# Residual through the product, separate rstd groups and a new priority table in a two-block kernel

## The chip, the cores and the metric

The kernel runs on one core of a Trainium2 chip. The metric is the device time of one execution in microseconds (us); the number compared is the median of several runs. The engines are TensorE (PE in the profile, with its weight loads as PEld), VectorE (DVE), ScalarE (ACT), GpSimd (POOL) and the sync engine (SP), which issues most of the DMAs.

## What is computed

Two residual blocks over x of 2048 rows and 512 columns, in bf16. The first is linear attention with 32 heads of 16 columns, the second a gated MLP that mixes along the sequence:

```python
def _A_ref(x, wqkv, wo):
    q, k, v = ...                       # x @ wqkv, split in 32 heads of 16
    phi = lambda t: jnp.where(t > 0, t + 1, jnp.exp(t)) + 1e-06
    pq, pk = (phi(q), phi(k))
    kv = einsum('bhsd,bhse->bhde', pk, v); z = einsum('bhsd->bhd', pk)
    o = einsum('bhqd,bhde->bhqe', pq, kv) / (einsum('bhqd,bhd->bhq', pq, z)[..., None] + 1e-06)
    return merge_heads(o) @ wo
def _B_ref(x, w_in, w_sp, b_sp, w_out):  # F = 1792, Fh = 896
    z = gelu_tanh(x @ w_in); z1 = z[..., :Fh]; z2 = _layernorm(z[..., Fh:])
    g = einsum('ts,bsf->btf', w_sp, z2) + b_sp[None, :, None]
    return (z1 * g) @ w_out
h = x + _A_ref(_layernorm(x), A_wqkv, A_wo)
h2 = h + _B_ref(_layernorm(h), B_w_in, B_w_sp, B_b_sp, B_w_out)
```

## The kernel before

All of x, the weights and the intermediates stay in SBUF. The sequence is 16 tiles of 128 rows, eight pairs (p), four groups of 512 rows (gq or tg). PSUM is a pool of eight banks of 128 x 512 fp32; four of them hold the accumulator `acc` until the k·v sums are done.

The kernel is written as a list of operations (`op`), each with its engine, an estimated cost, what it reads and writes, and a priority. A list scheduler (`schedule`, L185) then fixes the order on each engine: at each step it takes, per engine, the candidates that can start soonest by the estimates, and among those that could start within a small patience (0.1 or 0.2 us) of the engine's being free, the one with the lowest priority number. `NUDGE` (L372) is a table of numbers that are added to the priorities in the order in which the operations are listed; operations past its end get nothing. So the order of everything on each engine, the sync engine's DMA queue among it, depends on the priorities, the table and the cost estimates. `_waits` derives the semaphores from the resulting order.

The stages in the order of time:

- *Start.* Loads of x, k's weights, v's and q's; the first five of the 64 transposed loads of w_sp (WSP0 = 5); ten products on zeros (`spin`, L617).
- *First layernorm* (L657 to L685). Per x tile: statistics (`stats`, L624), aggregate (`aggr`, L628); per group of tiles of `LN1` one rstd by ScalarE, Ln then Exp (`rstd_of`, L638 and L640); then the normalised tile by VectorE (`normalise`, L652) or ScalarE (L679). `LN1` has the groups [0], [1], [2, 3] and then fours.
- *Transposes of the normalised x* (`transpose_pair`, L689): pairs below XDMA = 2 by TensorE (L704) and a ScalarE copy out of PSUM (L715), the others by DMA transposes on the sync queue (L693). After the first one of tile 0 one product on zeros fills in (L711).
- *k and q* (`k_proj` L749, `q_proj` L783), each followed by `phi`: exp on ScalarE (L721), a VectorE pass (L725), and a last VectorE pass that either reads PSUM again (L737) or, for pairs below FR = 2, adds a ReLU that ScalarE wrote (L724, L736).
- *k·v* (L769): the products of the normalised x with phi(k), summed over all tiles in `acc`; for pairs below AS = 6 as one operation per tile, for later pairs as one operation per tile and half of the output (h).
- *Handover*: column sums of phi(k) (L804 to L821), the small products that make the merged matrix `mw` (L831 to L865), the denominators (`den`, L876 to L883), their spreading over columns (`spread_den`, L893 and L899), the scaling of phi(q) (`scale_pq`, L915 and L919).
- *h* (L937 to L967), in units: tiles 0 and 1 alone, then pairs. Four products per tile (L948), the residual added by VectorE straight from PSUM into the tile of x (L953), statistics, aggregate, rstd, normalised tile (L652). The rstd comes from ScalarE for units that begin below LNACT = 2 and from GpSimd (`rstd_pow`, L645 and L647) for the others. Tiles 0 and 1 are transposed by TensorE, the others by DMA (HDMA = 1).
- *Second block*: z2 (L976, Gelu at L985, statistics at L992 or L1000), z1 (L1021, L1026), the mixing product (L1051) with bias and gate on VectorE (L1057, L1060), the output product (L1071), residual (L1076) and store.

ScalarE uses two function tables: one with Ln and Exp at the start, one for Gelu. The list `last_lnexp` holds ScalarE's last Ln and Exp operations; all Gelus are listed after them.

Of the kernel before, what the change touches and what calls it, by code (L numbers as in the profile page):

```python
# [7 lines left out]
ACT = mybir.ActivationFunctionType  # L8
ALU = mybir.AluOpType

P = 128
# [98 lines left out]
class Program:  # L110
# [259 lines left out]


NUDGE = [  # L372
# [29 lines left out]
]  # L402


# [1 line left out]
def bass_sequential_preLN__linear_attn_block__mixer_gmlp__prompt_kernel(  # L406
# [16 lines left out]
    NT, KD, KF, NG = S // P, D // P, FH // P, S // GW  # L423
    TPG = GW // P
    NP = NT // 2
    assert D == 512 and KD == 4 and NG == 4 and FH == KF * P and 512 < FH <= 1024
    WARM, XDMA, HDMA, LNACT = 10, 2, 1, 2
    FILL = 1
    AS, FR, FQ, N0, WSP0 = 6, 2, 0, 4, 5
    WV, WQ, NA, KA, QE, QI = 8.5, 4, 1, 35, 3, 15  # L430
    WSP1 = 8
    DB, DC, SPP, PK, ZD = 6, 7, 8, 0.3, 1
# [23 lines left out]
    x = View(s_x, 0, [NT, D], BF16)  # L456
# [32 lines left out]
    ident = small([P], BF16)  # L489
# [34 lines left out]
    def bank(i):  # L524
        return lambda a: a[:, i, :]
# [11 lines left out]
    op = g.op  # L537
# [3 lines left out]
    def act_c(n, ps=True, ptr=0):  # L541
        return 0.15 + 0.00085 * n + 0.09 * ptr

    def dve_c(n, ps=True, mode=1):
        return 0.06 + 0.00112 * n / mode
# [108 lines left out]
           r=[src, m, rs], w=[dst], prio=prio)  # L654


    LN1 = [[0], [1], [2, 3], [4, 5, 6, 7], [8, 9, 10, 11], [12, 13, 14, 15]]  # L657
    last_lnexp = []
    xn_t = {}
    for grp in LN1:  # L660
# [94 lines left out]
    for p in range(NP):  # L755
# [5 lines left out]
        for h in ((None,) if p < AS else (0, 1)):  # L761
            for n in (2 * p, 2 * p + 1):
# [3 lines left out]
                def mm(e, n=n, l=l, hs=hs):  # L766
                    for g_ in hs:
                        for c in range(KD):
                            i = e.matmul(acc(xk(g_, c)).ap(), lhsT=l.ap()[:, c * P:(c + 1) * P],  # L769
                                         rhs=pk.ap[:, n, g_ * HW:(g_ + 1) * HW], start=False,  # L770
                                         stop=(n == NT - 1 and c % 2 == 1))
                    return i
# [165 lines left out]
    for u in UNITS:  # L938
        k, n0 = len(u), u[0]
        pr = B0 + 5 * n0  # L940
        scale_pq(u, pr - SCP, r0)
        t = Tile(PS, k)
        for ti, n in enumerate(u):
            l = pqT[:, n * P:(n + 1) * P]

            def mm(e, t=t, ti=ti, l=l):
                for c in range(KD):
                    i = e.matmul(t(bank(ti)).ap(), lhsT=l.ap()[:, c, :], rhs=mw[c, :].ap(), start=(c == 0),  # L948
                                 stop=(c == KD - 1))
                return i  # L950
            op("pe", 4 * MM, mm, r=[l, mw.all()], w=[t()], prio=pr)
        d = x[n0:n0 + k, :]
        op("dve", dve_c(512 * k), lambda e, t=t, d=d: e.tensor_tensor(d.ap(), t().ap(), d.ap(), ALU.add),  # L953
           r=[t(), d], w=[d], prio=pr)
        for n in u:
            stats(x[n, :], Row(st_h, n), pr + 1)
        for n in u:
            aggr(Row(st_h, n), 6, pr + 1)
        rs = small([k], FP32)
        var = st_h[n0:n0 + k, 7]  # L960
        if n0 < LNACT:
            last_lnexp.append(rstd_of(var, rs.all(), pr + 2))
        else:
            rstd_pow(var, rs.all(), pr + 2, k)
        for i, n in enumerate(u):
            t = hn_t[n] = Tile(XN)
            normalise(t(), x[n, :], Row(st_h, n), 6, rs[i:i + 1], pr + 3)  # L967
# [178 lines left out]
```

## Time and profile before

| what | value |
|---|---|
| median of 3 runs | 248.45 us (247.92 to 248.77) |
| the profiled execution's own time | 248.1 us |
| its span, first to last instruction | 246.4 us |
| VectorE, ScalarE, GpSimd busy | 129.6, 88.1, 27.0 us |
| HBM read, written | 7.47 MB, 2.10 MB |

All times in the profile are of one execution on the chip. L followed by a number is a line of the kernel. A name such as `xT_pq_z` is a buffer; buffers are shared by tensors that live at different times (xT, phi(q) and z1 here; the normalised x, phi(k) and z2 in `pk_xn_z`; q, k, v weights, the spread denominators and a part of w_sp in `wqkv_wsp`; x and later h in `xh`). In rows by groups, the number after the bar is busy time in us, then the mean of one instruction in ns, then the engine's idle time just before such instructions and what ended it. SPq means the sync engine's queue of DMA issues.

### The profile page before, as it was taken

Reading aid. Unit: us, or ns where it says so; the run is one execution under the profiler, and the core shown is the slowest. Engines: PE = TensorE matmul, PEld = TensorE weight load, DVE = VectorE, ACT = ScalarE, POOL = GpSimd, SP = SyncE. Lnnn points to the kernel's source line nnn. Section 1 sums busy time; section 2 is a strip of 40 time slices with the busy share of each in tenths; the row PEclk is TensorE's granted clock in tenths of the full one; section 3 lists DMA queues with packets and bytes.
Section 4 is the critical chain, followed back from the end, with each engine's and each line's share of the span. In section 5 each row is a group of like instructions: output and inputs, shape, how many; then the busy total and the mean of one; then the engine's idle time right before and its main releaser. Section 6 shows DMA issues by size and latency. Waiting matters only on the chain.

```text
span 246.4 us, 3157 instructions
## 1 busy us (share of the span) xinstructions
PE 238.0 (97%) x1220; PEld 115.7 (47%) x1242; DVE 129.6 (53%) x247; ACT 88.1 (36%) x132; POOL 27.0 (11%) x73
## 2 busy tenths in 40 slices
PE   7799999999899999999999999999999999999995
PEld 3355565554354445454444444444444444444443
DVE  4998776669999996043033322352322523323443
ACT  3797583379767468988640000000000000000000
POOL 7100010100024444134200000000000000000000
PEclk9999999999999999999999999999999999999999
DMA  7993327999722043455474444111000110000022
GB/s 208 356 175 70 67 39 190 218 307 226 133 43 45 17 91 70 101 88 107 92 104 87 96 98 104 24 43 43 0 3 0 43 43 0 3 0 0 0 85 88
DMA packets 56015, 21.58 MB, mean 88 GB/s; under 512 B 49504, under 2 KB 55264, under 8 KB 56000
## 3 DMA queue, kind: packets, MB, share of 16 engines
q1 hardware_dynamic: 55072, 17.84, 33.9%
q0 software_dynamic: 656, 3.28, 4.2%
q10 hardware_dynamic: 272, 0.26, 0.3%
q8 instruction: 10, 0.16, 0.3%
q14 instruction: 5, 0.04, 0.1%
HBM read 7.47 MB, written 2.10 MB: 39 GB/s over the span
## 4 chain that ended last, share of the span: by engine, by line
PE 88%; ACT 4%; DVE 3%; DMA 3%; issue 1%; SPq 0%
PE ps L1051 39%; PE ps L976 10%; PE ps L1071 10%; PE ps L1021 10%; PE ps L749 4%; PE ps L948 4%; PE ps L769 4%; PE ps L783 4%; DMA xT_pq_z<-pk_xn_z 3%; PE ps L617 2%; ACT e L721 2%; ACT pk_xn_z L679 1%; DVE small L624 1%; DVE xh L953 1%; DVE xT_pq_z L919 1%
## 5 line engine op out<-in xcount | busy, mean ns | idle before, releaser
L1051 PE MATMUL ps<-wsp,pk_xn_z 128*128 128x512 bf16 x329 | 72.8, 379 | 0.4
L1057 DVE TENSOR_TENSOR r<-ps,e 128x512 bf16<-128x512 f32 x28 | 19.4, 692 | 65.2 <-PE ps L1051 65.2
L1051 PEld LDWEIGHTS ps<-wsp,pk_xn_z 128*128 128x128 bf16 x336 | 32.9, 98 | 39.6
L976 PE MATMUL ps<-win,hT 128*128 128x384 bf16 (+1 forms) x126 | 25.7, 352 | 0.1
L1021 PE MATMUL ps<-hT,win 128*128 128x512 bf16 x110 | 25.5, 379 | 0.1
L1071 PE MATMUL ps<-wout,xT_pq_z 128*128 128x512 bf16 (+1 forms) x117 | 24.4, 366 | 0.1
L1051 PE MATMUL ps<-wqkv_wsp,pk_xn_z 128*128 128x512 bf16 x110 | 24.2, 379 | 0.1
L624 DVE BATCH_NORM_STATS2 small<-xh 128x6 f32<-128x512 bf16 x32 | 21.4, 678 | 2.8 <-DMA xh<-in_A_x_dram 2.7
L721 ACT ACTIVATE e<-ps 128x1024 bf16<-128x1024 f32 x16 | 16.4, 1022 | 14.9 <-PE ps L783 10.6
L976 PEld LDWEIGHTS ps<-win,hT 128*128 128x128 bf16 x128 | 12.5, 98 | 12.2
L1071 PEld LDWEIGHTS ps<-wout,xT_pq_z 128*128 128x128 bf16 x119 | 11.6, 98 | 12.8
L985 ACT ACTIVATE pk_xn_z<-ps 128x896 bf16<-128x896 f32 x16 | 14.6, 915 | 7.8 <-PE ps L976 7.7
L1076 DVE TENSOR_TENSOR r<-ps,xh 128x512 bf16<-128x512 f32 (+1 forms) x17 | 11.2, 660 | 11.3 <-PE ps L1071 11.2
L1051 PEld LDWEIGHTS ps<-wqkv_wsp,pk_xn_z 128*128 128x128 bf16 x112 | 10.9, 98 | 13.2
L1021 PEld LDWEIGHTS ps<-hT,win 128*128 128x128 bf16 x112 | 10.9, 98 | 12.6
L783 PE MATMUL ps<-xT_pq_z,wqkv_wsp 128*128 128x512 bf16 x62 | 14.7, 379 | 1.7 <-ACT xT_pq_z L715 1.6
L948 PE MATMUL ps<-pk_xn_z,xT_pq_z 128*128 128x512 bf16 x62 | 15.0, 379 | 1.1 <-DVE xT_pq_z L919 0.7
L1026 ACT ACTIVATE xT_pq_z<-ps 128x1024 bf16<-128x1024 f32 x14 | 14.2, 1020 | 4.7 <-PE ps L1021 4.7
L749 PE MATMUL ps<-wqkv_wsp,xT_pq_z 128*128 128x512 bf16 x62 | 15.1, 380 | 0.5
L769 PE MATMUL ps<-pk_xn_z 128*128 128x256 bf16 x128 | 15.4, 273 | 0.0
L769 PEld LDWEIGHTS ps<-pk_xn_z 128*128 128x128 bf16 x128 | 12.4, 98 | 3.3 <-issue 0.4
L992 ACT ACTIVATE r<-pk_xn_z,small 128x896 bf16<-128x896 bf16 x12 | 12.4, 1037 | 1.7 <-POOL small L990 1.6
(85 smaller groups left out, 188.5 us busy)
## 6 DMA issues: line engine op xcount, KB each, us to landing
out_dram<-r SPq DMA_DIRECT2D x15, 128.0 KB, 1.7
xh<-in_A_x_dram SPq DMA_DIRECT2D x7, 256.0 KB, 4.9
win<-in_B_w_in_dram POOLq DMA_DIRECT2D x1, 1792.0 KB, 8.3
wqkv_wsp<-in_A_wqkv_dram SPq DMA_DIRECT2D x2, 512.0 KB, 7.0
wout<-in_B_w_out_dram POOLq DMA_DIRECT2D x1, 896.0 KB, 6.1
wsp<-in_B_w_sp_dram SPq DMA_TRANSPOSE x48, 3.3
wqkv_wsp<-in_A_wo_dram POOLq DMA_DIRECT2D x1, 512.0 KB, 4.8
e<-in_B_b_sp_dram SPq DMA_DIRECT2D x1, 512.0 KB, 7.2
```

What stands on the lines that cost most here:

```text
L624: op("dve", dve_c(512), lambda e: e.bn_stats(s6.ap(), src.ap()), r=[src], w=[s6], prio=prio)
L721: op("act", act_c(1024), lambda e: e.activation(e_().ap(), t(flat).ap(), ACT.Exp), r=[t()], w=[e_()], prio=prio)
L749: i = e.matmul(t(bank(ti)).ap(), lhsT=lhs.ap()[:, c, :], rhs=rhs.ap()[:, c, :], start=(c == 0), stop=(c == KD - 1))
L769: i = e.matmul(acc(xk(g_, c)).ap(), lhsT=l.ap()[:, c * P:(c + 1) * P], rhs=pk.ap[:, n, g_ * HW:(g_ + 1) * HW], start=False, stop=(n == NT ...
L783: r_ = e.matmul(t(bank(i)).ap(), lhsT=lhs.ap()[:, c, :], rhs=rhs.ap()[:, c, :], start=(c == 0), stop=(c == KD - 1))
L948: i = e.matmul(t(bank(ti)).ap(), lhsT=l.ap()[:, c, :], rhs=mw[c, :].ap(), start=(c == 0), stop=(c == KD - 1))
L976: k = e.matmul(t(bank(i)).ap()[:, 0:b - a], lhsT=l.ap()[:, c, :], rhs=win[c, a:b].ap(), start=(c == 0), stop=(c == KD - 1))
L985: op("act", act_c(FH, ptr=by_act), lambda e, t=t, d=d, acc={"accum_out": m.ap()} if by_act else {}: e.activation(d.ap(), t(flat).ap()[:, 0 ...
L1021: k = e.matmul(t(bank(i)).ap(), lhsT=l.ap()[:, c, :], rhs=r_.ap()[:, c, :], start=(c == 0), stop=(c == KD - 1))
L1051: k = e.matmul(t(bank(0)).ap(), lhsT=l.ap()[:, s - a, :], rhs=r_.ap()[:, s - a, :], start=(s == 0), stop=(s == NT - 1))
L1057: op("dve", dve_c(512), lambda e: e.tensor_tensor(gb().ap(), t(bank(0)).ap(), bsp().ap()[:, tg * GW:(tg + 1) * GW], ALU.add), r=[t(), bsp( ...
L1071: k = e.matmul(t(bank(0)).ap()[:, 0:z - a], lhsT=l.ap()[:, fc, :], rhs=w_.ap()[:, fc, :], start=(fc == 0), stop=(fc == KF - 1))
```

## The change

- The residual of h tiles 0 and 1 (units that begin below RP = 2): TensorE adds a fifth product, the unit matrix times the tile of x, to the same PSUM accumulation, and ScalarE copies the sum into the tile of x. VectorE's add stays for the other units.
- `LN1` gets the groups [0], [1], [2], [3] and then fours (LNG = 1): x tiles 2 and 3 have an rstd of their own.
- LNACT goes from 2 to 4: the rstd of the unit of h tiles 2 and 3 comes from ScalarE's Ln and Exp, and joins `last_lnexp`.
- AS goes from 6 to 5 (pair 5's k·v products are split by halves too), FR from 2 to 1 (pair 1's phi reads PSUM a second time in place of a ReLU by ScalarE). N2 is a new name that nothing uses.
- `NUDGE` is another table throughout. It is longer (616 numbers for 567): the operation list has three more ahead of the second block, and the new table reaches past the w_sp loads, whose entries are 0, to the first five of the mixing products.

```diff
 NUDGE = [
-    0, 0, 0, 0, 0, 0, 0, 0, 0, 0, 0, 0, 0, 0, 0, 0, 0, 0, 45, 0, 0, 0, 0, 0, 0, 0, 0, 0, 0, 0, 0, 0, 0, 0, 0, 0,
-    0, 0, 0, 0, 0, -36, -33, -25.5, -16, -70.5, 13.5, -141.5, 11, -16.5, 7, 0, 15.5, 20.5, 215, -111, -107.5,
...
+    0, 0, 0, 0, 0, 0, 0, 0, 0, 0, 0, 0, 0, 0, 0, 0, 0, 0, 744.5, 0, 0, 0, 0, 0, 0, 0, 0, 0, 0, 0, 0, 0, 0, 0, 0, 0,
+    0, 0, 0, 0, 0, 0, -32.5, -314.5, -29.5, -30.5, -46.5, -1011, -221, 65, 118.5, -254.5, 4, -460, 5, 108.5, 32,
...
-    WARM, XDMA, HDMA, LNACT = 10, 2, 1, 2
-    FILL = 1
-    AS, FR, FQ, N0, WSP0 = 6, 2, 0, 4, 5
+    WARM, XDMA, HDMA, LNACT = 10, 2, 1, 4
+    FILL, LNG, RP, N2 = 1, 1, 2, 0
+    AS, FR, FQ, N0, WSP0 = 5, 1, 0, 4, 5
...
-    LN1 = [[0], [1], [2, 3], [4, 5, 6, 7], [8, 9, 10, 11], [12, 13, 14, 15]]
+    cuts = [[0, 1, 2, 4, 8, 12], [0, 1, 2, 3, 4, 8, 12], [0, 1, 2, 3, 4, 6, 8, 12], [0, 1, 2, 4, 6, 8, 10, 12, 14]][LNG] + [NT]
+    LN1 = [list(range(a, z)) for a, z in zip(cuts, cuts[1:])]
...
-            l = pqT[:, n * P:(n + 1) * P]
-
-            def mm(e, t=t, ti=ti, l=l):
+            l, h = pqT[:, n * P:(n + 1) * P], x[n, :]
+            by_pe = n0 < RP
+
+            def mm(e, t=t, ti=ti, l=l, h=h, by_pe=by_pe):
                 for c in range(KD):
                     i = e.matmul(t(bank(ti)).ap(), lhsT=l.ap()[:, c, :], rhs=mw[c, :].ap(), start=(c == 0),
-                                 stop=(c == KD - 1))
+                                 stop=(c == KD - 1 and not by_pe))
+                if by_pe:
+                    i = e.matmul(t(bank(ti)).ap(), lhsT=ident.all().ap(), rhs=h.ap(), start=False, stop=True)
                 return i
-            op("pe", 4 * MM, mm, r=[l, mw.all()], w=[t()], prio=pr)
+            op("pe", (4 + by_pe) * MM, mm, r=[l, mw.all()] + ([ident.all(), h] if by_pe else []), w=[t()], prio=pr)
         d = x[n0:n0 + k, :]
-        op("dve", dve_c(512 * k), lambda e, t=t, d=d: e.tensor_tensor(d.ap(), t().ap(), d.ap(), ALU.add),
-           r=[t(), d], w=[d], prio=pr)
+        if n0 < RP:
+            op("act", act_c(512 * k), lambda e, t=t, d=d: e.activation(d.ap(), t().ap(), ACT.Copy), r=[t()], w=[d], prio=pr)
+        else:
+            op("dve", dve_c(512 * k), lambda e, t=t, d=d: e.tensor_tensor(d.ap(), t().ap(), d.ap(), ALU.add),
+               r=[t(), d], w=[d], prio=pr)
```

57 rows, old and new, of the table NUDGE are left out of this document.

## The prediction

> **What bounds the kernel now.** I read the granted clock first, then the page's busy shares, then the busy time by stretches of ten microseconds, then TensorE's waits, and last the chain of waits in order of time.
>
> ```profile
> core 0: 246.4 us, clock 0.999
> ```
> ```profile
> PE 238.0 (97%) x1220; PEld 115.7 (47%) x1242; DVE 129.6 (53%) x247; ACT 88.1 (36%) x132; POOL 27.0 (11%) x73
> ```
> The clock is full, so no time is lost or won there. TensorE (PE) is busy for 238.0 of 246.4 us. Busy time can hide pipelining, so the waits have to say where TensorE was dry. They are few:
>
> ```profile
> PE ps L783 <- ACT xT_pq_z L715: 1.6, 1, 1.6
> ...
> PE ps L948 <- DVE xT_pq_z L919: 0.7, 2, 0.5
> PE ps L915 <- ACT pk_xn_z L861: 0.5, 1, 0.5
> PE ps L948 <- DVE small L628: 0.3, 1, 0.3
> PE ps L915 <- DVE hn L844: 0.2, 1, 0.2
> ```
> Columns: total, number of waits, longest. One wait of 1.6 us stands at the first layernorm; the other four, 1.7 us together, stand where the first block hands over to the second. The chain places them (start, length, what):
>
> ```profile
> 8.88 1.02 ACT e L721
> 9.91 0.99 ACT xT_pq_z L715 x2
> ...
> 10.94 1.92 PE ps L783 x8
> ...
> 16.75 2.52 DMA xT_pq_z<-pk_xn_z
> ...
> 19.32 1.04 PE ps L749 x4
> 20.36 1.75 PE ps L769 x16
> ...
> 27.30 1.73 PE ps L783 x8
> ...
> 60.21 0.69 DVE xh L953
> 60.90 1.19 DVE small L624 x2
> ...
> 66.91 0.19 DVE small L628
> ...
> 67.11 1.02 PE ps L948 x4
> ...
> 69.44 3.03 PE ps L976 x16
> ...
> 243.93 0.42 DVE r L1076
> ```
> Three places are to be seen. At 8.88 ScalarE evaluates exp of pair 0 for 1.02 us, and only then copies the transposes of x tiles 2 and 3 (L715, 0.99); TensorE starts again at 10.94. At 16.75 to 19.27 the chain runs through a DMA: the transpose of x tile 5, which L749 needs at 19.32. From 60.21 to 67.10 it runs through VectorE: residual add (L953), statistics, aggregates. From 69.44 to 243.9 it is TensorE's work nearly without a break. So an earlier start of that long part comes out at the end one for one, and nothing else counts.
>
> ```profile
> 10.00:20.00 10.00, 8.75 (x47) 4.48 (x49) 9.08 (x25) 8.29 (x12) 0.00 (x0) 1.00 0.94 205
> ...
> 50.00:60.00 10.00, 9.34 (x96) 5.10 (x97) 7.93 (x11) 8.74 (x11) 0.00 (x0) 1.00 1.30 301
> 60.00:70.00 10.00, 9.02 (x52) 3.90 (x52) 9.83 (x21) 7.12 (x12) 0.96 (x2) 1.00 0.52 95
> 70.00:80.00 10.00, 9.95 (x51) 4.92 (x51) 9.39 (x18) 7.54 (x14) 3.50 (x8) 1.00 0.27 54
> ```
> Columns after the stretch and its length: busy time of PE, weight loads, VectorE, ScalarE, GpSimd. In 60 to 70 VectorE is full (9.83), ScalarE has 2.9 us to spare, TensorE about 1.
>
> **The change part by part.** Its prices are in the groups by shape (after the count: busy us in all, and the mean of one in ns):
>
> ```profile
> L737 DVE SCALAR_TENSOR_TENSOR pk_xn_z<-ps,e 128x1024 bf16<-128x1024 f32 x6 | 7.3, 1224 | 0.1
> ...
> L647 POOL TENSOR_TENSOR small<-small 128x2 f32<-128x2 f32 x7 | 5.1, 726 | 0.6
> ...
> L724 ACT ACTIVATE e<-ps 128x1024 bf16<-128x1024 f32 x2 | 2.1, 1030 | 0.0
> ...
> L645 POOL TENSOR_SCALAR small<-small 128x2 f32<-128x2 f32 x7 | 2.0, 292 | 26.6 <-DVE small L628 26.3 <-POOL small L647 0.2 <-POOL small L995 0.2
> ...
> L953 DVE TENSOR_TENSOR xh<-ps,xh 128x512 bf16<-128x512 f32 x2 | 1.4, 688 | 0.1
> ...
> L736 DVE TENSOR_TENSOR pk_xn_z<-e 128x1024 bf16<-128x1024 bf16 x2 | 1.4, 684 | 0.0
> ...
> L638 ACT ACTIVATE small<-small 128x1 f32<-128x1 f32 x4 | 1.2, 295 | 2.2 <-DVE small L628 2.2
> ...
> L640 ACT ACTIVATE small<-small 128x1 f32<-128x1 f32 x4 | 0.8, 203 | 0.1
> ...
> L808 ACT ACTIVATE hn<-ps 128x512 bf16<-128x512 f32 x1 | 0.6, 597 | 0.0
> ```
> *First layernorm* (own rstd for x tiles 2 and 3, one ReLU less, new order). The split adds one Ln and one Exp, 0.295 + 0.203 = 0.50 us of ScalarE. FR from 2 to 1 takes the ReLU of pair 1 away, 1.03 us of ScalarE, and puts a 1.224 us pass on VectorE in place of 0.684, so +0.54 there. ScalarE nets -0.53. With its own rstd, tile 2 can be normalised and transposed without tile 3, and its copy no longer has to stand behind the exp of pair 0: in the new table the two copies have priorities -26 and -22.5 (before: -74.5 and -122) against 18.5 for that exp (before: -116), the lower first. Taken alone this is worth up to the whole 1.6 us. But what is late next is already visible:
>
> ```profile
> 6.96 8.44 SPq L566 DMA_TRANSPOSE wsp<-in_B_w_sp_dram  x5
> 15.43 22.98 SPq L693 DMA_TRANSPOSE xT_pq_z<-pk_xn_z  x12
> ```
> ```profile
> 13.04 0.41 DVE L652 TENSOR_SCALAR pk_xn_z<-xh,small 128x512 bf16<-128x512 bf16 x1
> ```
> The sync queue issues five w_sp transposes until 15.40, and only then those of x tiles 4 and up, though tile 4 was normalised at 13.45. WSP0 stays 5, and the change moves nothing past that queue's front, so tile 5 lands near 19.27 as before (16.75 + 2.52). What TensorE can gain is then what it can do ahead of that landing instead of after it: the k·v group of pair 1 (the 1.75 us at 20.36). Its input is pair 1's k, whose exp (1.02, as for pair 0) and last VectorE pass (now 1.22 us) fit if the k product of pair 1 runs early. The gain lies between 0 (that group is not pulled forward) and 1.75. I take 1.25, nearer the upper end, because the input of the group is about 1.6 us earlier, less the 0.54 that VectorE pays extra in a stretch where it is busy 9.08 of 10.
>
> *Handover, 50 to 59* (AS from 6 to 5). Pair 5's k·v products are cut in halves of the output, so that the first half can close sooner. No product is added. The waits there are 0.5 + 0.2 = 0.7 us; I take a gain of 0.2, between a loss of 0.3 (the new order opens a wait like the 0.3 one) and 0.7.
>
> *Residual of h tiles 0 and 1* (RP = 2). VectorE loses two adds, 2 x 0.688 = 1.38 us. TensorE gains two products of 512 columns. By the group of eight at 27.30, one is 1.73 / 8 = 0.216, so +0.43 us, and it stands on the chain in full. ScalarE gets two PSUM copies of the same shape as L808, 2 x 0.597 = 1.19 us. The chain's VectorE stretch from 60.21 to 67.10 shrinks by at most the 1.38, but TensorE is dry in it for only the 0.7 + 0.3 = 1.0 us of the two L948 waits, so the most that comes out is 1.0 - 0.43 = 0.57 of gain. The other end is given by ScalarE's queue:
>
> ```profile
> 59.44 1.92 ACT L899 ACTIVATE wqkv_wsp<-ps 128x1024 bf16<-128x1024 f32 x2
> ```
> The two copies fall due exactly where ScalarE moves the spread reciprocals (L899), which the scaling L919 of later tiles waits for. If these go back by 1.19 and nothing is won, the cost is 1.19 + 0.43 = 1.62. I take a gain of 0.3, nearer the good end because VectorE and not ScalarE is the full engine there.
>
> The Trainium skill ("ScalarE: Activation LUTs", Rules for kernel authors) speaks against this edit: add and mul belong on VectorE, which per element is up to about three times faster than ScalarE in bf16. The rows above say otherwise for a source in PSUM, 597 ns on ScalarE against 688 on VectorE; by the page's factor two copies would cost 3 x 1.38 = 4.1 us of ScalarE, and the handover would lose instead of gain.
>
> *rstd of h tiles 2 and 3 on ScalarE* (LNACT 2 to 4). Ln and Exp, about 0.50, in place of GpSimd's 0.292 + 0.726 = 1.02; the normalised tiles come half a microsecond sooner.
>
> ```profile
> 69.04 0.72 DVE L652 TENSOR_SCALAR hn<-xh,small 128x512 bf16<-128x512 bf16 x2
> ```
> ```profile
> 70.09 1.28 ACT L985 ACT_TABLE_LOAD   x1
> 72.50 0.92 ACT L985 ACTIVATE pk_xn_z<-ps 128x896 bf16<-128x896 f32 x1 [1.13 <-PE ps L976]
> ```
> I cost it at nothing. TensorE has 3.03 us of L976 work at 69.44 that needs tiles 0 and 1 alone, and it covers the half microsecond either way. All Ln and Exp must precede the table load for Gelu at 70.09, so these two may push it back by 0.5; ScalarE then still idles before its first Gelu, which waited 1.13 us for TensorE. Without that cover it would cost the 0.5.
>
> *The priority table* changes the order everywhere. After 69.44 TensorE has no wait to remove, so there a new order can only lose; I put it at 0, bounded by a loss of 0.5 (half a microsecond is about the size of the waits that the old order left).
>
> Sum, against the profiled execution: 248.1 - 1.25 - 0.2 - 0.3 = 246.35. That execution is 246.4 of span and 1.7 around it, and lies 0.35 below the median of the three runs (248.45). On the scale of the median: 248.45 - 1.75 = 246.7.
>
> **The rivals.**
>
> *A, the forecast: both stalls shrink.* 246.7. Its own range: gains at most 1.75 + 0.7 + 0.57 = 3.0, which is 245.4, and at least about 0.9, which is 247.5.
>
> *B, hidden anyway.* TensorE starts sooner than 10.94 and then waits longer for x tiles 4 and 5, because the sync queue decides. For it: the transposes stand behind the five w_sp loads. Against it: 1.75 us of k·v work that can be moved. Gain 0 there and 0.2 from the handover less nothing: 248.3.
>
> *C, ScalarE takes VectorE's place (the slower side).* Place: ScalarE's queue from 59.4 on. Price: 1.19 us of copies ahead of the L899 moves, plus 0.43 of products. It decides as soon as the first pair of L899 ends more than about 1 us after the 61.36 of now, because TensorE then has only h products that wait for L919, and the long part starts late. For it: ScalarE is already at 8.74 of 10 in 50 to 60. Against it: it idles 2.9 us in 60 to 70. If it also stays without the first layernorm's gain: 248.45 + 1.62 = 250.1. The Trainium skill ("TensorE: Matmul & The Clock Gate", Architectural detail) says that ScalarE's queue is strictly first in, first out, so that a late copy would hold up all behind it; no row here contradicts that.
>
> *D, the first edit does not do what it says.* The copies of tiles 2 and 3 still come after the exp, since tile 3's statistics end no sooner; the 1.6 us wait stays. Only 0.5 from the handover: 247.95.
>
> **How the numbers follow.** A measurement of this kernel can tell about 0.3% from no change, 0.75 us, so faster means below 247.7 and slower above 249.2. A has 0.54 (faster 0.52, within 0.02), B 0.12 (0.02 faster, 0.08 within, 0.02 slower), C 0.24 (0.01 within, 0.23 slower), D 0.10 (0.06 faster, 0.03 within, 0.01 slower). C has that much because every engine is near full at the handover and the whole order is new. Together: faster 0.60, within 0.14, slower 0.26. The range goes from 244.8, a little below A's best, to 250.1, C's price; C's worse half, about 0.12, and 0.06 below are left out.
>
> **What would show it.** Right: the wait of L783 or L749 on L715 falls from 1.6 to under 0.6; the residual copies appear on ScalarE at about 597 ns; the two L948 waits of 1.0 us together shrink; the first L976 group starts near 67.7 instead of 69.44, and the end moves with it. Wrong: a wait of TensorE on an x transpose that grows by what L715 gave up (B); L899 ending past 62.4 and L976 starting at 70 or later (C); L721 still ahead of L715 (D); or new waits of TensorE after 70, which I put at none.

## The result, and the profile after

| | before | changed |
|---|---|---|
| median of 5 runs each | 248.44 us (247.92 to 248.77) | 246.68 us (246.51 to 247.21) |
| ratio, with its 95% interval | | 0.9936 [0.9918, 0.9954] |
| the profiled execution's own time | 248.1 us | 246.68 us |
| its span, with the granted clock | 246.4 us, 0.999 | 245.0 us, 0.999 |

The changed kernel is faster by 1.76 us. The two profiled executions differ by 1.42 us, and this is what the traces have to account for. In the changed kernel the line numbers are two or three higher at first and four to nine higher behind the h products: the transposes are L707, k L752, k·v L772, q L786, column sums L807, spread denominators L896, the h product L952, the unit-matrix product L955, ScalarE's copy of it L960, z2 L985.

The busy shares and TensorE's waits (total, number of waits, longest) of the changed kernel:

```profile
PE 238.0 (97%) x1222; PEld 115.3 (47%) x1244; DVE 129.2 (53%) x245; ACT 88.4 (36%) x137; POOL 24.9 (10%) x71
```
```profile
PE ps L707 <- DVE pk_xn_z L654: 1.4, 2, 1.0
```

TensorE is busy for the same 238.0 us; only idle time has gone. The wait of 1.6 us on ScalarE's copy (L715) is no longer there, nor any of the four at the handover and the h products. New are the wait for VectorE's normalised tiles and one of 0.54 us for a DMA transpose of x, which stands in the timeline below. The same stretches as in the prediction, by busy time of TensorE, weight loads, VectorE, ScalarE and GpSimd:

```profile
50.00:60.00 10.00, 9.93 (x79) 4.88 (x77) 8.06 (x12) 8.54 (x11) 0.00 (x0) 1.00 1.33 249
60.00:70.00 10.00, 9.95 (x57) 4.50 (x57) 10.00 (x20) 7.33 (x14) 0.00 (x0) 1.00 0.73 158
```

From 50 to 70 TensorE went from 9.34 and 9.02 to 9.93 and 9.95 of 10. It is now full through the handover and the h products.

Where the time came from is read off TensorE's timeline (start, length, what, and in brackets the idle time before it), at places that both kernels have. Before:

```profile
5.49 0.63 PE L704 MATMUL ps<-small,pk_xn_z 128*128 128x128 bf16 x4
...
16.15 1.89 PE L783 MATMUL ps<-xT_pq_z,wqkv_wsp 128*128 128x512 bf16 x8
18.17 2.18 PE L749 MATMUL ps<-wqkv_wsp,xT_pq_z 128*128 128x512 bf16 x8
20.20 1.91 PE L769 MATMUL ps<-pk_xn_z 128*128 128x256 bf16 x16
...
50.06 1.05 PE L804 MATMUL ps<-pk_xn_z,small 128*32 128x512 bf16 x16
...
57.84 1.04 PE L948 MATMUL ps<-pk_xn_z,xT_pq_z 128*128 128x512 bf16 x4
...
69.28 3.03 PE L976 MATMUL ps<-win,hT 128*128 128x512 bf16 x15
```

The changed kernel, and the last line of its chain of waits:

```profile
6.74 0.40 PE L707 MATMUL ps<-small,pk_xn_z 128*128 128x128 bf16 x4 [1.05 <-DVE pk_xn_z L654]
...
15.74 1.89 PE L786 MATMUL ps<-xT_pq_z,wqkv_wsp 128*128 128x512 bf16 x8
18.17 2.10 PE L752 MATMUL ps<-wqkv_wsp,xT_pq_z 128*128 128x512 bf16 x8 [0.54 <-DMA xT_pq_z<-pk_xn_z]
20.11 1.91 PE L772 MATMUL ps<-pk_xn_z 128*128 128x256 bf16 x16
...
47.95 1.05 PE L807 MATMUL ps<-pk_xn_z,small 128*32 128x512 bf16 x16
...
54.46 1.89 PE L786 MATMUL ps<-xT_pq_z,wqkv_wsp 128*128 128x512 bf16 x8
56.19 0.39 PE L918 MATMUL ps<-r,sel 128*128 128x128 bf16 x4
...
56.83 1.04 PE L952 MATMUL ps<-pk_xn_z,xT_pq_z 128*128 128x512 bf16 x4
...
67.42 1.03 PE L985 MATMUL ps<-win,hT 128*128 128x512 bf16 x4
```
```profile
242.50 0.42 DVE r L1085
```

One group of eight q products now stands behind the column sums, at 54.46, and takes 1.73 us (54.46 to 56.19); it is added to the first part and taken from the second, so that equal work is compared. (Two more small groups change places around the first h product, one of spreading products and one for the denominators; they take 0.33 us each and cancel.)

| stretch | before | changed | difference |
|---|---|---|---|
| start to the column sums, q group counted in | 50.06 | 47.95 + 1.73 = 49.68 | -0.38 |
| column sums to the first h product, q group left out | 7.78 | 8.88 - 1.73 = 7.15 | -0.63 |
| first h product to the first z2 product | 11.44 | 10.59 | -0.85 |
| first z2 product to VectorE's last residual (243.93, 242.50) | 174.65 | 175.08 | +0.43 |
| sum | | | -1.43 |

The sum is right and its division isn't what was forecast: the first layernorm, which was to bring 1.25 us, brought almost nothing by 20 us (20.20 against 20.11), and the handover with the h products brought most of it. The last row is in part a loan: of the three groups of spreading products (before at 58.81, 61.83 and 64.58, all ahead of z2) the last now comes at 79.61, behind the first z2 product. A group costs 0.33 us of TensorE wherever it stands (58.81 to the next product at 59.14 before).

### The profile page after: what moved, and what is told of

Its sections match the earlier page's. It is cut to its first block, busy times and chain, and to the rows that moved or that the text cites. A ratio compares the mean times of both kernels' runs of the same rounds, so it can differ in the third digit from the quotient of the medians.

```text
span 245.0 us, 3170 instructions
## 1 busy us (share of the span) xinstructions
PE 238.0 (97%) x1222; PEld 115.3 (47%) x1244; DVE 129.2 (53%) x245; ACT 88.4 (36%) x137; POOL 24.9 (10%) x71
## 4 chain that ended last, share of the span: by engine, by line
PE 87%; DMA 4%; DVE 3%; ACT 2%; issue 1%; POOL 1%; SPq 1%; POOLq 0%; DVEq 0%
PE ps L1060 39%; PE ps L1080 10%; PE ps L985 8%; PE ps L1030 7%; PE ps L952 6%; PE ps L772 5%; PE ps L752 5%; PE ps L786 4%; DMA xh<-in_A_x_dram 2%; DMA xT_pq_z<-pk_xn_z 1%; DMA hT<-hn 1%; DVE small L626 1%; SPq L696 1%; POOL small L649 1%; PE ps L879 0%
## 5 line engine op out<-in xcount | busy, mean ns | idle before, releaser
L1060 PEld LDWEIGHTS ps<-wsp,pk_xn_z 128*128 128x128 bf16 x336 | 32.9, 98 | 39.6
L985 PE MATMUL ps<-win,hT 128*128 128x384 bf16 (+1 forms) x124 | 25.5, 352 | 0.2
L985 PEld LDWEIGHTS ps<-win,hT 128*128 128x128 bf16 x128 | 12.5, 98 | 12.5
L772 PE MATMUL ps<-pk_xn_z 128*128 128x256 bf16 x128 | 15.7, 273 | 0.0
L752 PE MATMUL ps<-wqkv_wsp,xT_pq_z 128*128 128x512 bf16 x61 | 14.8, 379 | 0.8 <-DMA xT_pq_z<-pk_xn_z 0.5
L952 PE MATMUL ps<-pk_xn_z,xT_pq_z 128*128 128x512 bf16 x63 | 15.3, 380 | 0.1
L786 PE MATMUL ps<-xT_pq_z,wqkv_wsp 128*128 128x512 bf16 x63 | 15.1, 379 | 0.1
L772 PEld LDWEIGHTS ps<-pk_xn_z 128*128 128x128 bf16 x128 | 12.3, 98 | 3.7 <-issue 0.7
L654 DVE TENSOR_SCALAR pk_xn_z<-pk_xn_z,small 128x896 bf16<-128x896 bf16 x16 | 7.2, 502 | 12.6 <-POOL small L649 12.6
```

What stands on the lines that cost most here:

```text
L752: i = e.matmul(t(bank(ti)).ap(), lhsT=lhs.ap()[:, c, :], rhs=rhs.ap()[:, c, :], start=(c == 0), stop=(c == KD - 1))
L786: r_ = e.matmul(t(bank(i)).ap(), lhsT=lhs.ap()[:, c, :], rhs=rhs.ap()[:, c, :], start=(c == 0), stop=(c == KD - 1))
L985: k = e.matmul(t(bank(i)).ap()[:, 0:b - a], lhsT=l.ap()[:, c, :], rhs=win[c, a:b].ap(), start=(c == 0), stop=(c == KD - 1))
L1060: k = e.matmul(t(bank(0)).ap(), lhsT=l.ap()[:, s - a, :], rhs=r_.ap()[:, s - a, :], start=(s == 0), stop=(s == NT - 1))
```

## The experiments

To move one thing and nothing else, the order on each engine was written out in most runs: the table goes, and the scheduler takes its operations (numbered as they are listed) in a given order.

```diff
-    def schedule(self, nudge=()):
-        for o, d in zip(self.ops, nudge):
-            o.prio += d
+    def schedule(self, fixed):
...
+                    if o.seq != fixed[e][len(order[e])]:
+                        continue
...
-    g.schedule(NUDGE)
+    g.schedule(ORDER)
```

Lines are then 14 higher than in the changed kernel (k·v L786, h product L966, z2 L999). The runs were taken in three sets, 1 and 3 on one chip and 2 on another, each in five rounds beside the kernel before on the same chip. A median is of 12 executions, of 8 for the run with the x transposes ahead and of 6 for the one with both moves:

| run | set | median, us | ratio to before |
|---|---|---|---|
| changed kernel, order written out | 3 | 247.22 | 0.9972 [0.9950, 0.9993] |
| first stage of the change alone | 1 | 248.45 | 0.9990 [0.9970, 1.0010] |
| rear of the change alone | 1 | 248.53 | 1.0008 [0.9985, 1.0032] |
| the same, four k·v products in another order | 2 | 247.13 | 0.9964 [0.9942, 0.9987] |
| change without its residual edit | 1 | 247.90 | 0.9978 [0.9958, 0.9999] |
| residual edit on the old order | 1 | 248.57 | 1.0003 [0.9982, 1.0024] |
| change, normalising started earlier | 2 | 247.16 | 0.9956 [0.9935, 0.9976] |
| change, k·v of pair 1 pulled forward | 2 | 248.12 | 0.9987 [0.9963, 1.0012] |
| change, x transposes ahead in the sync queue | 3 | 246.41 | 0.9936 [0.9914, 0.9957] |
| change, normalising earlier and x transposes ahead | 2 | 245.81 | 0.9899 [0.9873, 0.9924] |
| change with LNACT 2 | 3 | 247.34 | 0.9954 [0.9936, 0.9971] |
| change with x tiles 2 and 3 on one rstd | 3 | 247.32 | 0.9967 [0.9941, 0.9993] |

The changed kernel's program with its order written out measured 0.9972 where the changed kernel had measured 0.9936, above the 0.993 to 0.995 that was expected. So between sets of runs two or three parts in a thousand are not settled, and readings that need less rest on the traces.

### The changed kernel's order written out

> The changed kernel once more, its engine orders written out instead of derived from the table, as the reference for the three runs beside it: 246.7, ratio to before 0.993 to 0.995, by every theory.

It is the reference for the three runs of its set. In its profiled execution the stretch from the first h product to z2 is 57.38 to 67.97, again 10.59, and TensorE waits 0.6 us for the transpose of x tile 7, a wait that the changed kernel's own profile hasn't. When a DMA transpose lands varies between executions of one program, enough to make a wait of 0.6 us or none.

### Which half of the change earned it

First stage of the change (LNG, FR, AS, its order up to the column sums) with the old order behind it:

```diff
-    FILL, LNG, RP, N2 = 1, 1, 2, 0
+    FILL, LNG, RP, N2 = 1, 1, 0, 0
-    WARM, XDMA, HDMA, LNACT = 10, 2, 1, 4
+    WARM, XDMA, HDMA, LNACT = 10, 2, 1, 2
```

> The first layernorm, k, q and k.v stage in the changed kernel's order and with its groups (LNG, AS, FR); everything from the column sums of phi(k) on as in the kernel before, residual on VectorE, rstd of h tiles 2 and 3 on GpSimd. Theory 1 (the ledger of TensorE's waits: the first stage wins almost nothing, because the first tile starts 1.25 us later and the rest is eaten by the wait for x tile 4): gain of 0 to 0.5 us on the kernel before, about 248.1. Theory 2 (as predicted: the first stage gives 1.25 of the 1.75 us): about 247.2.

0.999: nothing that can be told from zero. Its waits of TensorE:

```profile
PE ps L721 <- DVE pk_xn_z L668: 1.6, 2, 1.3
PE ps L766 <- DMA xT_pq_z<-pk_xn_z: 1.4, 2, 0.7
...
PE ps L966 <- DVE xT_pq_z L936: 0.7, 2, 0.5
PE ps L932 <- ACT pk_xn_z L878: 0.5, 1, 0.5
```

The waits of the handover and the h products are back in their old size, and in place of the 1.6 us on ScalarE's copy stand 1.6 on VectorE's normalised tiles and 1.4 on DMA transposes.

The opposite: the old first stage, the rest of the change behind it.

```diff
-    FILL, LNG, RP, N2 = 1, 1, 2, 0
-    AS, FR, FQ, N0, WSP0 = 5, 1, 0, 4, 5
+    FILL, LNG, RP, N2 = 1, 0, 2, 0
+    AS, FR, FQ, N0, WSP0 = 6, 2, 0, 4, 5
```

> The other half: first layernorm, k, q and k.v as in the kernel before; from the column sums on the changed kernel's order, with the residual of h tiles 0 and 1 by product and ScalarE and the rstd of h tiles 2 and 3 on ScalarE. Theory 1: this half carries the gain, 1.0 to 1.5 us, about 247.2. Theory 2: 0.5 us, about 247.9.

1.0008: nothing either, though the residual edit is in it. A cause shows in ScalarE's copy of the first half of the k·v sums (L834, with the order written out L848). In the changed kernel:

```profile
50.01 1.02 ACT L834 ACTIVATE wqkv_wsp<-ps 128x1024 bf16<-128x1024 f32 x1 [0.37 <-PE ps L772]
```

In this run, with the column sums and the first h product on TensorE:

```profile
51.20 1.02 ACT L848 ACTIVATE wqkv_wsp<-ps 128x1024 bf16<-128x1024 f32 x1 [0.90 <-PE ps L786]
```
```profile
48.60 1.05 PE L821 MATMUL ps<-pk_xn_z,small 128*32 128x512 bf16 x16
...
58.73 1.04 PE L966 MATMUL ps<-pk_xn_z,xT_pq_z 128*128 128x512 bf16 x4
```

The old first stage ended with a product of the second half ahead of the last two of the first half, so the first half closed late. From the column sums to the first h product this takes 58.73 - 48.60 = 10.13, where the changed kernel has 8.88. The next run alters those four operations alone:

```diff
 ORDER["pe"]
-    ..., 176, 177, 239, 187, 185, 241, 186, 265, 188, ...
+    ..., 176, 177, 239, 185, 186, 241, 187, 265, 188, ...
```

> The rear half again (first layernorm, k, q, k.v as before, the rest in the changed kernel's order, with its residual and rstd), but the last four k.v products in the order that the changed kernel's handover needs (both of the first output half, then both of the second). If the handover alone carries the gain: 247.2 (1.0 to 1.4 us faster than before). If it needs the changed first stage as well: 248.2 or later.

```profile
48.56 1.05 PE L821 MATMUL ps<-pk_xn_z,small 128*32 128x512 bf16 x16
...
57.45 1.04 PE L966 MATMUL ps<-pk_xn_z,xT_pq_z 128*128 128x512 bf16 x4
```

The ratio falls from 1.0008 to 0.9964, 1.1 us, and the stretch is 57.45 - 48.56 = 8.89, that of the changed kernel. The two runs are of different sets and their intervals overlap by a hair (0.9985 and 0.9987), so the cause rests on the traces: four operations alone differ, and the stretch loses 1.24 us. (The profiled execution of this run took 251.96 us, with a wait of 2.93 us for a DMA transpose of h ahead of the z2 products at 75.88; only these earlier times are read from it.) With the old first stage, this version is where the changed program was in the set after it (0.9972). So the rear of the change, with its order of the last half-products, earned the time, and the first stage earned none that a measurement shows.

### The residual edit

Taken out of the change: RP = 0, and VectorE's two adds put back into its order, each just ahead of its tile's statistics.

```diff
-    FILL, LNG, RP, N2 = 1, 1, 2, 0
+    FILL, LNG, RP, N2 = 1, 1, 0, 0
```

> The changed kernel with all engine orders kept, but the residual of h tiles 0 and 1 undone: no fifth product, and VectorE's add stands in its queue just before each tile's statistics. As predicted the residual edit is worth 0.3: about 247.0. If it is the main gain of the handover it is worth 0.8 or more: 247.5 or later, with a wait of TensorE on VectorE in the h products. If only the new order matters, the two products saved show as 0.4 us less: about 246.3.

TensorE's timeline of this run, then VectorE's:

```profile
57.83 1.90 PE L966 MATMUL ps<-pk_xn_z,xT_pq_z 128*128 128x512 bf16 x8
60.18 1.04 PE L966 MATMUL ps<-pk_xn_z,xT_pq_z 128*128 128x512 bf16 x4 [0.45 <-DVE xT_pq_z L754]
...
63.62 2.77 PE L966 MATMUL ps<-pk_xn_z,xT_pq_z 128*128 128x512 bf16 x11 [0.77 <-DVE xT_pq_z L936]
...
69.27 1.03 PE L999 MATMUL ps<-win,hT 128*128 128x512 bf16 x4
```
```profile
60.04 0.68 DVE L976 TENSOR_TENSOR xh<-ps,xh 128x512 bf16<-128x512 f32 x1
...
62.91 1.26 DVE L936 TENSOR_TENSOR xT_pq_z<-xT_pq_z,wqkv_wsp 128x1024 bf16<-128x1024 bf16 x2
```

The same scaling in the changed kernel:

```profile
60.74 1.29 DVE L922 TENSOR_TENSOR xT_pq_z<-xT_pq_z,wqkv_wsp 128x1024 bf16<-128x1024 bf16 x2
```

Counted from the first h product, the scaling starts after 62.91 - 57.83 = 5.08 us with the adds on VectorE, and after 60.74 - 56.83 = 3.91 without them: 1.17 later, nearly the two adds (0.68 us for the one shown). TensorE waits 0.45 + 0.77 = 1.22 us for VectorE. The stretch to z2 is 69.27 - 57.83 = 11.44 against 10.59: in this order the edit is worth 0.85 us, its products paid. (In this execution the first four k products took 1.91 us where the changed kernel's took 1.03, so nothing ahead of 57.83 is read from it.) By the times the worth isn't so sharp: 0.9978 against 0.9936 or 0.9972 is between 0.06% and 0.42%, 0.15 to 1.0 us.

The edit alone, on the old order, with ScalarE's copies set one ahead of its first move of spread denominators (L899) and one between the first two:

```diff
-    FILL, LNG, RP, N2 = 1, 1, 2, 0
-    AS, FR, FQ, N0, WSP0 = 5, 1, 0, 4, 5
+    FILL, LNG, RP, N2 = 1, 0, 2, 0
+    AS, FR, FQ, N0, WSP0 = 6, 2, 0, 4, 5
-    WARM, XDMA, HDMA, LNACT = 10, 2, 1, 4
+    WARM, XDMA, HDMA, LNACT = 10, 2, 1, 2
```

> The kernel before with its orders kept, and only the residual of h tiles 0 and 1 moved: fifth product on TensorE, ScalarE's copies standing one ahead of the first and one between the first two moves of the spread reciprocals. If the edit needs its own order: slower by 0.5 to 1.6 us (249 to 250), because the moves of the spread reciprocals and with them the scaling of tiles 4 and 5 come later. If VectorE's load alone decides: faster by 0.3 to 0.6 us (about 248.0).

```profile
58.71 1.04 PE L966 MATMUL ps<-pk_xn_z,xT_pq_z 128*128 128x512 bf16 x4
...
68.35 1.02 PE L966 MATMUL ps<-pk_xn_z,xT_pq_z 128*128 128x512 bf16 x4 [0.30 <-ACT wqkv_wsp L916]
...
70.52 1.68 PE L999 MATMUL ps<-win,hT 128*128 128x512 bf16 x8
```

11.81 us from the first h product to z2, 0.37 more than the 11.44 of before. The last wait of that stretch used to be on VectorE (L948 on L628, 0.30); now it is 0.30 on ScalarE's move of the denominators. TensorE's waits of the stretch fall only from 0.98 to 0.79 us (0.33, 0.16 and 0.30). VectorE's relief is mostly taken up by ScalarE's queue, the two products stay to be paid, and the ratio is 1.0003. The edit paid in the order that sends less through that queue at that time: the changed kernel has one of the three spreading groups ahead of the first h product and one behind z2.

### Why the first layernorm gave nothing

In the changed kernel the transposes of x tile 0 start at 6.74, where they started at 5.49. VectorE's timeline:

```profile
5.47 0.69 DVE L626 BATCH_NORM_STATS2 small<-xh 128x6 f32<-128x512 bf16 x1 [0.73 <-DMA xh<-in_A_x_dram]
...
6.30 0.38 DVE L654 TENSOR_SCALAR pk_xn_z<-xh,small 128x512 bf16<-128x512 bf16 x1
```

The new order has the statistics of x tile 2 ahead of the normalised tile 0, and that tile's load ends only at 5.47. The first experiment here puts the normalised tiles 0 and 1 ahead of those statistics (three moves on VectorE, two on ScalarE).

```diff
 ORDER["dve"]
-    ..., 41, 46, 42, 47, 51, 52, 45, 56, 50, 57, ...
+    ..., 41, 42, 46, 47, 45, 51, 50, 52, 56, 57, ...
 ORDER["act"]
-    ..., 48, 53, 49, 54, 109, 58, ...
+    ..., 48, 49, 109, 53, 54, 58, ...
```

> The changed kernel, with x tile 0's and tile 1's normalisation put back ahead of the statistics of tile 2, which wait for a load (three VectorE operations and two ScalarE operations moved, nothing else). If the late start costs the end: 245.6 (1.1 us faster than the changed kernel's 246.7). If the sync queue decides, because x tile 4 lands no sooner: no change, 246.5 to 246.8, and TensorE's wait for the DMA transpose grows from 0.5 to about 1.6.

```profile
5.48 0.63 PE L721 MATMUL ps<-small,pk_xn_z 128*128 128x128 bf16 x4
...
15.47 1.89 PE L800 MATMUL ps<-xT_pq_z,wqkv_wsp 128*128 128x512 bf16 x8
18.25 2.16 PE L766 MATMUL ps<-wqkv_wsp,xT_pq_z 128*128 128x512 bf16 x8 [0.89 <-DMA xT_pq_z<-pk_xn_z]
```

TensorE starts 1.26 us earlier, but waits of 0.5 for a normalised tile and 0.3 for an exp, and first transposes that take 0.63 us instead of 0.40, leave 0.27 of it at the last q products ahead of x tile 4 (15.47 against 15.74). Those 0.27 are lost to the DMA, whose wait grows from 0.54 to 0.89. The kernel before is at 16.15 there, and all three begin on x tile 4 at 18.17 to 18.25: how early TensorE comes doesn't matter, the landing does. By times 0.9956 stands beside 0.9936 and 0.9972 for the changed kernel, no gain that can be told.

The second one does what the prediction took for the source of its 1.25 us: the k·v group of pair 1 ahead of the k products that need the DMA.

```diff
 ORDER["pe"]
-    ..., 216, 217, 133, 134, 129, 130, 142, ...
+    ..., 216, 217, 129, 130, 133, 134, 142, ...
```

> The changed kernel with one move: the two k.v products of pair 1 ahead of the k product of x tile 5. This is the gain that the prediction counted on (1.75 us of work ahead of the landing of x tile 5). If it is there: the wait of 0.5 goes, 246.0 to 246.3. If pair 1's phi is not ready by 19, or the later k product delays the next exp: 246.7 or later.

```profile
17.46 1.91 PE L786 MATMUL ps<-pk_xn_z 128*128 128x256 bf16 x16
...
23.97 1.25 PE L800 MATMUL ps<-xT_pq_z,wqkv_wsp 128*128 128x512 bf16 x5 [1.15 <-DVE pk_xn_z L754]
```
```profile
22.70 1.22 DVE L754 SCALAR_TENSOR_TENSOR pk_xn_z<-ps,e 128x1024 bf16<-128x1024 f32 x1
```

The group does start at 17.46 instead of 20.11, and the wait for the DMA is gone. But the k products of pair 2 come later, so their phi does, and VectorE's last pass, which frees their PSUM, ends at 23.92 (22.70 + 1.22). TensorE then waits 1.15 us, and its column sums come at 48.35 instead of 47.95: what was gained at 18 us is owed at 24 us. The median is 248.12, 0.9987, but the profiled execution took 247.10. Five of the twelve took 246.91 to 247.31 and seven 248.04 to 249.23; the trace is of the first kind, and what the others lost isn't known.

Two runs move the sync queue instead: the DMA transposes of x tiles 4 and 5 ahead of the fourth w_sp load, those of tiles 6 and 7 ahead of the fifth, once with the changed kernel and once with the earlier start added.

```diff
 ORDER["sp"]
-    ..., 15, 16, 17, 131, 132, 140, 141, 150, ...
+    ..., 15, 131, 132, 16, 140, 141, 17, 150, ...
```

> The changed kernel with only the sync queue's order changed: transposes of x tiles 4 and 5 ahead of the last two of the five w_sp loads. If the queue alone held the first stage: 0.5 to 0.7 us faster than the run e_after, the size of its wait for x tile 4 (0.5), about 246.0. If both the late start and the queue hold it, as e_start (no gain) and e_start_queue (0.4% below the changed kernel's ratio) together suggest: between 245.9 and 246.5, since the late start then decides. If the queue does nothing: 246.7.

> The changed kernel with the earlier start of the run e_start and, on the sync queue, the transposes of x tiles 4 and 5 ahead of the last two of the five w_sp loads. If the queue is what holds the first stage: x tile 4 lands near 16 instead of 18, TensorE's wait for it goes, and the time falls by 1.0 to 1.4 us, to 245.3 to 245.7. If the normalised tile 4 or pair 1's exp decides instead: within 0.3 of the run e_start.

The queue alone gives 0.9936, by medians 0.8 us better than the changed program of its set (0.9972; the two intervals overlap by 0.0007). With the earlier start it is 0.9899, clear of the earlier start alone (0.9956): 245.81 us (245.47 to 246.37), below every run of the changed kernel. It has the lowest median of all. Its sync queue, and TensorE where it used to wait:

```profile
13.66 2.53 SPq L710 DMA_TRANSPOSE xT_pq_z<-pk_xn_z  x2
```
```profile
16.04 1.89 PE L800 MATMUL ps<-xT_pq_z,wqkv_wsp 128*128 128x512 bf16 x8
17.77 1.89 PE L766 MATMUL ps<-wqkv_wsp,xT_pq_z 128*128 128x512 bf16 x8
...
47.33 1.05 PE L821 MATMUL ps<-pk_xn_z,small 128*32 128x512 bf16 x16
```

The first transpose of x is issued at 13.66, where it was 15.35 in the changed kernel and 15.43 before. TensorE doesn't wait for x, and the column sums come at 47.33 instead of 47.95. So the sync queue held the first stage: moved ahead on top of the earlier start, its transposes are worth 1.35 us by the medians of one set (247.16 to 245.81) and 0.76 us at the column sums of the two traces (48.09 to 47.33). That the earlier start adds to the queue is not shown: in this trace the q products ahead of x tile 4 start at 16.04, later than the changed kernel's 15.74, and the intervals with and without the start ([0.9873, 0.9924] and [0.9914, 0.9957]) overlap.

### The two small edits

```diff
-    WARM, XDMA, HDMA, LNACT = 10, 2, 1, 4
+    WARM, XDMA, HDMA, LNACT = 10, 2, 1, 2
```

> The changed kernel with the rstd of h tiles 2 and 3 back on GpSimd (LNACT 2). As predicted it costs nothing either way: within 0.3 us of the run e_after. If the half microsecond that it takes longer is on the path: 0.5 slower, with a wait of TensorE on the transposed h tile 2.

```diff
-    FILL, LNG, RP, N2 = 1, 1, 2, 0
+    FILL, LNG, RP, N2 = 1, 0, 2, 0
```

> The changed kernel with x tiles 2 and 3 sharing one rstd again (LNG 0), every engine's order kept otherwise. The prediction took this split for what removes the 1.6 us wait. By the queue theory the 0.5 us that tile 2 comes later is hidden by the wait for x tile 4: within 0.3 us of the run e_after, that wait of 0.5 getting smaller. If the split is on the path: 0.5 to 1.0 slower.

247.34 and 247.32 us, beside 247.22 for the changed program of the same set. By the times neither the rstd of h tiles 2 and 3 on ScalarE nor the own rstd of x tiles 2 and 3 can be told from nothing. (The run with LNACT 2 keeps the table; the orders that it gives on TensorE and the sync queue are the changed kernel's, and on VectorE three operations change places.) But the trace with LNACT 2 has the wait that was named as the sign of a cost:

```profile
PE ps L985 <- DMA hT<-hn: 0.6, 1, 0.6
```

The changed kernel's has none there. One trace doesn't settle it, since the run with one rstd, which has LNACT 4, also waits 0.25 us for a transposed h tile at that place. In the trace of the run with one rstd, with the rest of the change as it is, the old wait on ScalarE's copy doesn't come back: the order took it away, not the split. AS and FR were not taken back one by one.

## Why the prediction was right in its sum and wrong in its parts

*First layernorm, -1.25: mis-sized and its mechanism refuted.* The wait on L715 did go, and the copies of tiles 2 and 3 (9.18) do stand ahead of the exp of pair 0 (10.26), so rival D was rightly put low. But the change came out at -0.09 by 20 us. The prediction also left TensorE's start where it was; the new table puts it 1.25 us later (6.74 for 5.49), and at the last q products ahead of x tile 4 TensorE is only 0.41 us ahead (15.74 for 16.15). Putting the start back added 0.27 there, not 1.26. The step that failed is "I take 1.25, nearer the upper end, because the input of the group is about 1.6 us earlier". The k·v group of pair 1 was not pulled forward, and when an experiment pulled it, a wait of 1.15 us for VectorE came five microseconds later. The step had looked at the next wait only; the operations that such a move delays need the same look. The 0.41 us went as rival B had it, hidden by the sync queue (18.17 in both). The other 0.30 of the stretch's 0.38 came where nothing was forecast: between 37.5 and 39.6 eight q products and the next k product lay 2.03 us apart before (37.54 to 39.57) and 1.73 after. The chain of waits before runs there through a DMA transpose of x, a row that the prediction didn't read:

```profile
34.46 4.98 DMA xT_pq_z<-pk_xn_z
```

It lands at 39.44, just ahead of the k products at 39.57. Two runs with the old first stage wait for such a transpose at the same place (0.26 us in the rear of the change alone, 0.40 with the residual edit on the old order), the changed kernel doesn't.

*Handover, -0.2: it gave -0.63.* The two waits there, 0.16 and 0.46 on the timeline, went entirely, the whole of the bound of 0.7. Splitting pair 5 isn't what mattered: the run with four k·v products in another order has AS = 6 and the changed kernel's stretch (8.89 for 8.88). The order of the last half-products was worth 1.24 us of it.

*Residual, -0.3: it gave about -0.55.* The bound was 1.0 of waits less 0.43 of products, 0.57. The waits before the h products went in full (0.52 + 0.16 + 0.30 = 0.98), the two products cost their 0.43, which leaves -0.55; the other 0.30 of the stretch's 0.85 is, within 0.03, the spreading group put off, paid after 70 us. The end of the range at which ScalarE's queue takes over was real as well: on the old order it turned the edit into +0.37. The argument for the good end, that VectorE and not ScalarE is the full engine there, held; what it lacked is that the order decides.

The copies took what their nearest row had said:

```profile
L960 ACT ACTIVATE xh<-ps 128x512 bf16<-128x512 f32 x2 | 1.2, 601 | 0.4 <-PE ps L955 0.4
```

601 ns, against 597 forecast and 688 of a VectorE add. The Trainium skill ("ScalarE: Activation LUTs", Rules for kernel authors) puts add and mul on VectorE, and gives its factor of about three in bf16 for operations with a single source in VectorE's 4x mode. The residual add has two sources, one of them fp32 in PSUM, so the 4.1 us that the prediction worked out by that factor was no price for this case; the rows were.

*LNACT at nothing:* held by the times, and the changed kernel has no wait there; with LNACT 2 one trace has a wait of 0.65 us on a transposed h tile, so the cover that the prediction counted on may not be whole. *Priority table after 69.44 at nothing, up to a loss of 0.5:* +0.43 was measured there. 0.33 of it is the spreading group, work put off and no new wait; the view of waits has none after 70, and the other 0.10 isn't traced.

So of a forecast of -1.25, -0.2 and -0.3 the traces show -0.38, -0.63 and -0.55 to -0.85, and +0.43 behind: the errors of the parts cancelled to 0.32 us (-1.43 for -1.75). That was luck, and a right sum is no proof of its terms.

Open: why the same program measured 0.9936 and 0.9972 in two sets, if not by chance, since the intervals meet ([0.9918, 0.9954] and [0.9950, 0.9993]). The landing of the x transposes varies between executions, and so does the clock (below): four of the twelve executions with the order written out have a mean granted clock of 0.993, none of the changed kernel's five. Neither was held still. Nor was the wait for PSUM in the run with the early k·v group taken away by another buffer.

## What to carry to other kernels

When a wait is removed, follow the operations that the new order delays as well as those it advances: here one group moved 2.65 us forward was paid back 5 us later by PSUM that came free late. Before an earlier start is priced, look for the next landing that the work needs: TensorE came to x tile 4 at three different times and began on it at the same one, and only moving the transfers in the sync queue changed that. That move was worth 1.35 us by medians and 0.76 by traces. Moving work from a full engine to an emptier one pays only if the order of the emptier one's queue is made for it; by the traces the same edit was worth 0.85 us in one order and cost 0.37 in another.

## What the runs showed of the hardware

*The granted clock can halve after a short idle stretch.* In the run with the x transposes ahead, TensorE was idle for 1.88 us before the first transposes, and its granted clock was 0.50 in the stretch after it. Its window (the figure after the five engines is the clock), then its timeline:

```profile
7.40:10.70 3.30, 3.01 (x17) 1.91 (x18) 3.30 (x9) 1.68 (x5) 0.00 (x0) 0.50 1.08 353
```
```profile
6.77 0.40 PE L721 MATMUL ps<-small,pk_xn_z 128*128 128x128 bf16 x4 [1.88 <-DVE pk_xn_z L668]
...
8.09 1.91 PE L766 MATMUL ps<-wqkv_wsp,xT_pq_z 128*128 128x512 bf16 x4
```

Four products took 1.91 us, where the changed kernel's took 1.03 at 7.89. The clock row doesn't mark every slow product: without the residual edit (at 8.06) and with one rstd (at 7.77) four products took 1.91 us too, and there it says 1.00.

The Trainium skill ("TensorE: Matmul & The Clock Gate", Part 1) has the clock fall back after at least one idle window of about 3.4 us. Here 1.88 us of idleness were followed by the fall, and the measurement decides. In the run with four k·v products in another order, the wait of 2.93 us that ended at 75.88 was followed by a clock of 0.50 between 77 and 79.

An execution with such a fall has a mean granted clock of 0.993 or less. There are 19 of them in 85 executions of programs whose first transposes start at 6.46 us or later in their traces, and 8 in 149 of those with the earlier start, the kernel before among them. Where in these executions the clock fell is known only for the two that have a trace, so that the late start brings the falls on is likely and not shown. In the run with the x transposes ahead, the two such executions took 247.28 and 247.67 us, the six others 245.74 to 246.83.

*The sync queue is held by each DMA transpose.* Five w_sp loads took 8.05 us of it in the changed kernel, and two x transposes 2.53 in the fastest run, 1.26 each:

```profile
7.25 8.05 SPq L568 DMA_TRANSPOSE wsp<-in_B_w_sp_dram  x5
```

What stands in that queue ahead of a transpose delayed it by its whole issue, and this set when TensorE could pass 18 us.
